# Banks of PSUM assigned by hand, whole accumulators as side work, a shared score bank and x transposed by DMA, in a recurrent attention kernel

## The chip, the cores and the metric

One core of one Trainium2 chip. The time of a kernel is its device time in microseconds. The runs of one kernel lie within 0.5% of their median here. A ratio is the mean time of one kernel's fast runs over that of the other's fast runs of the same rounds, so it is not quite the ratio of the medians quoted beside it. Within a trace, times are counted from the start of the execution.

## The reference

A gate mixes two branches. Branch B is a layer norm and a two-layer MLP; it takes the first 108 us and the change leaves it alone. Branch A runs through the sequence in 64 segments of 32 rows, one after the other, because each hands eight rows of memory to the next:

```python
for s in range(64):
    h = concatenate([mem, x[:, 32*s : 32*s+32]])          # 8 + 32 rows of 512
    q, k, v = h @ Wq, h @ Wk, h @ Wv                      # 32 heads of 128
    p = softmax(where(mask, q @ k.T * 128**-0.5, -1e9))   # 40 x 40 per head
    o = (p @ v) @ Wo
    mem = o[:, :8]                                        # needed by the next s
    outs.append(o[:, 8:])
return g * concatenate(outs) + (1 - g) * B(x)             # g = sigmoid(x . gate_w)
```

## The kernel before

A step of the loop is one segment; a tile is four steps (128 rows of x). TensorE works on 32 rows at a time, with four column tiles side by side. Such a block holds the 8 memory rows and the first 24 rows of the segment. The last 8 rows of each of four segments ("left-over", names with L) do not depend on the memory; they are projected a tile ahead, as side work, which fills TensorE wherever a step would wait. The matmuls write into PSUM, of which the kernel uses eight banks. One is S, for the scores; the other seven go round in the order of the calls:

```python
pb = loop.enter_context(tc.tile_pool(name="pb", bufs=7, space=PSUM))
ps = loop.enter_context(tc.tile_pool(name="ps", bufs=1, space=PSUM))
def bank(shape, dtype=FP32):
    return pb.tile(shape, dtype, tag="b", name="b")

def x_tr(T, x_sb):                                # x tile T, transposed on TensorE
    xp = bank([P, KC, P], BF16)
    for kc in range(KC):
        nc.tensor.transpose(xp[:, kc, :], x_sb[:, kc * P:(kc + 1) * P], ident[:])
    def ev():                                     # VectorE copies it out, GpSimd picks GL
        ...

def filler(T):                                    # side work of a tile, in units of four matmuls
    if T + 1 < NT:
        for vb in range(2):
            yield from left_v(T + 1, vb)          # its result goes through DRAM to VL
        for hf in range(2):
            for t in range(2):
                yield from left_qk(T + 1, t, hf)
    if T >= 1:
        yield from wo_left(T - 1)
        yield from out_units(T - 1)               # also x_tr(T + 2), its load just before
```

The step, with cuts:

```python
            if s >= 1:
                prep_q(s)                         # GpSimd: QL -> QT columns 32:40
                x_mul(s - 1)                      # GpSimd: Px = E * R
            ...                                   # q, k: five banks, VectorE transposes,
                                                  # ScalarE (GpSimd for the third) casts to QT, KT
            scores(S, s)                          # TensorE, needs all of QT
            ...                                   # E = exp(S) on ScalarE, first sums sm
            run_fill(5)                           # five side units
            ...                                   # Pm; four banks Um <- Pm V, then VL
            sr = bank([P, NG, 32])                # late sums, and R = 1/sr on VectorE (1.75 us)
            run_fill(2)
        for half in range(2):
            wp = bank([P, 256])                   # Wo, two halves
            ...
        if live and s >= 1:
            av_x(s - 1)                           # four more banks <- Px V, then VL
        run_fill(1)
        if s + 1 < nseg:
            aT = bank([P, KC, M])                 # new memory, transposed by matmuls with Sel
            ...
            nc.vector.tensor_copy(out=hn[:, :, 0:M], in_=aT[:])
            S_next = mask_mm()                    # mask of the next step into S
        run_fill(1)
```

## Time and profile before

| | before |
|---|---|
| median | 921.3 us (three runs, 918.32 to 922.12) |
| TensorE busy | 832.7 us, 90% of the span |
| first step begins | 138.7 us |
| the four steps of an inner tile (medians) | 11.99, 12.02, 12.16, 11.54 us |
| last step begins, to the end | 25.3 us |

The row of steps is read from the timeline: a step begins with its first matmul of Wq with hT. The lines that carry the argument are in the prediction. A reader of such lines should take the distance between the starts of two matmuls, not their durations: matmuls are pipelined, and their ends are modelled.

### The profile page before, as it was taken

The numbers are of one execution on the slowest core, as the hardware profiler recorded it, in microseconds if no ns is written. First come the engines' busy times: TensorE is split into PE (matmuls) and PEld (weight loads), VectorE is DVE, ScalarE is ACT, GpSimd is POOL, SyncE is SP. The second block draws the span as 40 slices with busy tenths as digits, with TensorE's granted clock in tenths as the row PEclk, the third lists the DMA queues.
The fourth block names the chain that finished last, engine by engine and source line by source line (L and its number), as shares of the span: only waits on it lengthen the run. The fifth ranks groups of instructions, "written<-read, shape, count | busy, mean of one in ns | idle before, by whom it ended". The sixth has DMA issues, their size and how long they took to land.

```text
span 920.6 us, 49285 instructions
## 1 busy us (share of the span) xinstructions
PE 832.7 (90%) x22481; PEld 519.9 (56%) x22481; DVE 502.2 (55%) x999; ACT 443.2 (48%) x1252; POOL 257.1 (28%) x599
## 2 busy tenths in 40 slices
PE   1899738899999999999999999999999999999996
PEld 1566414555556566565656555656555566655554
DVE  4722214655556565556565656565656565655553
ACT  2666404454545445554544454555455545444453
POOL 1000172333333322333332323232323232323221
PEclk9999959999999999999999999999999999999998
DMA  9970001100000000010101000000000000000000
GB/s 281 421 260 1 7 1 31 27 9 26 15 27 15 27 16 26 10 32 10 32 5 37 5 27 14 28 14 23 19 21 21 15 27 15 27 15 21 10 4 17
DMA packets 29829, 37.77 MB, mean 41 GB/s; under 512 B 3592, under 2 KB 27504, under 8 KB 28080
## 3 DMA queue, kind: packets, MB, share of 16 engines
q1 hardware_dynamic: 29440, 34.30, 10.9%
q8 instruction: 178, 2.92, 1.3%
q0 software_dynamic: 176, 0.27, 0.2%
q14 instruction: 35, 0.29, 0.1%
HBM read 28.26 MB, written 6.29 MB: 38 GB/s over the span
## 4 chain that ended last, share of the span: by engine, by line
PE 81%; ACT 7%; issue 3%; DVE 3%; DMA 2%; POOL 2%; SPq 1%; ACTq 0%; POOLq 0%; DVEq 0%
PE b L269 32%; PE b L291 16%; PE b L280 12%; PE b L451 4%; PE bp L172 3%; PE hp L178 3%; ACT E L552 3%; PE b L456 2%; PE S L436 2%; PE b L566 1%; ACT wsb L590 1%; PE b L599 1%; PE b L555 1%; ACT UTT L511 1%; PE S L427 1%
## 5 line engine op out<-in xcount | busy, mean ns | idle before, releaser
L275 DVE STREAM_TRANSPOSE Tt<-b 128x512 f32<-128x512 f32 (+1 forms) x384 | 225.8, 613 | 97.4 <-PE b L269 85.1
L269 PEld LDWEIGHTS <-hT 128*32 128x32 bf16 x5120 | 134.1, 97 | 93.1 <-DVE hT L600 6.3
L291 PE MATMUL b<-Wo_sb,UTT 128*32 128x256 bf16 (+1 forms) x4736 | 166.4, 289 | 1.1 <-ACT UTT L511 0.8
L291 PEld LDWEIGHTS <-UTT 128*32 128x32 bf16 x4736 | 125.3, 98 | 26.9 <-issue 3.1
L269 PE MATMUL b<-Wq_sb,hT 128*32 128x512 bf16 x2048 | 132.9, 379 | 1.3
L280 PE MATMUL b<-Wv_sb,hT 128*32 128x512 bf16 x2048 | 133.9, 380 | 0.0
L269 PE MATMUL b<-Wk_sb,hT 128*32 128x256 bf16 (+1 forms) x3072 | 133.3, 308 | 0.0
L497 POOL TENSOR_TENSOR Px<-E,R 128x256 bf16<-128x256 bf16 x64 | 43.1, 674 | 258.1 <-DVE R L571 254.4
L571 DVE RECIPROCAL R<-b 128x256 f32<-128x256 f32 x64 | 112.0, 1749 | 4.2 <-PE b L567 4.2
L536 ACT CAST KT<-Tt 128x256 bf16<-128x256 f32 (+1 forms) x192 | 87.0, 476 | 54.1 <-DVE Tt L275 54.1
L536 POOL CAST QT<-Tt 128x512 bf16<-128x512 f32 x64 | 39.2, 612 | 189.7 <-DVE Tt L275 189.7
L590 ACT CAST wsb<-b 128x256 bf16<-128x256 f32 x66 | 24.6, 372 | 134.3 <-PE b L291 134.3
L536 ACT CAST QT<-Tt 128x512 bf16<-128x512 f32 x64 | 39.6, 618 | 98.7 <-DVE Tt L275 98.7
L511 ACT CAST UTT<-b 128x256 bf16<-128x256 f32 x256 | 77.0, 387 | 12.8 <-PE b L456 10.0
L559 DVE RECIPROCAL R<-b 128x64 f32<-128x64 f32 x64 | 35.7, 557 | 85.1 <-PE b L556 85.1
L280 PEld LDWEIGHTS <-hT 128*32 128x32 bf16 x2048 | 50.7, 96 | 28.2
L451 PEld LDWEIGHTS <-V 32*128 32x128 bf16 x4096 | 36.2, 91 | 50.8 <-DVE Pm L561 29.0
L600 DVE CAST hT<-b 128x32 bf16<-128x32 f32 x63 | 12.0, 191 | 90.3 <-PE b L599 90.3
L570 ACT CAST UTT<-b 128x64 bf16<-128x64 f32 x128 | 20.9, 215 | 77.5 <-PE b L456 77.5
L178 PE MATMUL hp<-yT,w_sb 128*128 128x256 bf16 (+1 forms) x352 | 52.5, 276 | 5.3 <-ACT hTm L179 3.5
L499 POOL TENSOR_TENSOR racc<-racc,R 128x320 f32<-128x320 f32 x64 | 55.1, 862 | 0.0
L179 ACT ACTIVATE hTm<-hp,b_sb 128x256 bf16<-128x256 f32 (+1 forms) x88 | 40.5, 470 | 29.2 <-PE hp L178 29.0
(110 smaller groups left out, 1087.1 us busy)
## 6 DMA issues: line engine op xcount, KB each, us to landing
Wq_sb<-in_A_Wq_dram SPq DMA_DIRECT2D x4, 1024.0 KB
Wk_sb<-in_A_Wk_dram SPq DMA_DIRECT2D x4, 1024.0 KB
Wv_sb<-in_A_Wv_dram SPq DMA_DIRECT2D x4, 1024.0 KB
Wo_sb<-in_A_Wo_dram SPq DMA_DIRECT2D x4, 1024.0 KB
vd<-vt SPq DMA_DIRECT2D x32, 128.0 KB
VL<-vd SPq DMA_DIRECT2D x256, 16.0 KB
out_dram<-o SPq DMA_DIRECT2D x16, 128.0 KB
xc<-in_A_x_dram SPq DMA_DIRECT2D x15, 128.0 KB
```

What stands on the lines that cost most here:

```text
L178: nc.tensor.matmul(hp[:rows, :], lhsT=w1_sb[:, kc, fc * P:fc * P + rows], rhs=yT[:, kc, :], start=(kc == 0), stop=(kc == KC - 1))
L179: nc.scalar.activation(out=hTm[:rows, fc, :], in_=hp[:rows, :], func=ACTF.Gelu_apprx_tanh, bias=b1_sb[:rows, fc:fc + 1], scale=1.0)
L269: nc.tensor.matmul(bk[32 * j:32 * j + 32, 0:n], lhsT=G[:, kc, :], rhs=W5[t][:, kc, h0:h1, j, :], start=(kc == 0), stop=(kc == KC - 1), til ...
L275: nc.vector.transpose(out=Tt[:, 0:n], in_=bk[:, 0:n])
L280: nc.tensor.matmul(bk[32 * j:32 * j + 32, :], lhsT=G[:, kc, :], rhs=Wv5[:, kc, 4 * vb:4 * vb + 4, j, :], start=(kc == 0), stop=(kc == KC - ...
L291: nc.tensor.matmul(bk[32 * g:32 * g + 32, :], lhsT=ut[:, i, j, c0:c0 + 32], rhs=Wo_sb[:, 4 * i + j, d0:d1], start=(j == 0 and i < 4), stop ...
L451: nc.tensor.matmul(U[j][:, i, :], lhsT=V[q, i, :], rhs=Pt[q, i, c_main:c_main + n], start=(i == 0), stop=False, skip_group_check=True, til ...
L497: nc.gpsimd.tensor_tensor(out=Px[:, :, 0:32], in0=E[:, :, 16:48], in1=Rr, op=ALU.mult)
L499: nc.gpsimd.tensor_tensor(out=racc[:], in0=racc[:], in1=R[:], op=ALU.add)
L511: nc.scalar.copy(out=UTT[T % 2][:, :, j, c0 + M:c0 + 40], in_=U[:])
L536: (nc.gpsimd.tensor_copy if bi == 2 else nc.scalar.copy)(out=dst, in_=Tv)
L571: nc.vector.reciprocal(out=R[:, 8 * NG:].rearrange("p (i q) -> p i q", q=32), in_=sr[:])
```

## The change

Its intent is to rid TensorE of waits for banks. Every accumulator gets a bank by number: 0 to 4 turn in a ring for the main work, 5 and 6 alternate for side work, and bank 7 holds mask and scores, later the late sums, and then, beside the next mask, the new memory. Side work becomes two whole accumulators in each step, with units placed four, two, one and one (one more in two of the places in step 3). As mask and memory share a bank, the mask moves ahead of the value product. And the transposes of x leave TensorE and VectorE for the DMA.

```diff
-    pb = loop.enter_context(tc.tile_pool(name="pb", bufs=7, space=PSUM))
-    ps = loop.enter_context(tc.tile_pool(name="ps", bufs=1, space=PSUM))
+    pb = loop.enter_context(tc.tile_pool(name="pb", bufs=1, space=PSUM))
+    def bank(k, shape, dtype=FP32):
+        return pb.tile(shape, dtype, tag=f"b{k}", name=f"b{k}")
...
     def x_load(T):
+        xT = cw.tile([P, KC, P], BF16, tag="xT", bufs=3, name="xT")
+        for kc in range(KC):
+            nc.sync.dma_start_transpose(xT[:, kc, :], x2[T * P:(T + 1) * P, kc * P:(kc + 1) * P])
+        xTs[T] = xT
+        GL = cw.tile([P, KC, 32], BF16, tag="GL", name="GL")
+        nc.gpsimd.tensor_copy(out=GL[:]..., in_=xT[:]...)
+        GLs[T] = GL
...
+        if si == 1 and T + 2 < NT:
+            x_load(T + 2)
+        if live:
+            B, S = S_next
+            na, nb, nc_, nd, ne = ring
+            ring = (nd, ne, na, nc_, nb)
             if s >= 2:
                 ux_out(s - 2)
+                flush(act_q)
...
             if s >= 1:
                 prep_q(s)
                 x_mul(s - 1)
...
-            run_fill(5)
+            run_fill(4 + (si == 3))
...
-            sr = bank([P, NG, 32])
+            sr = B[:, 0:NG * 32].rearrange("p (i q) -> p i q", q=32)
...
+        if s + 1 < nseg:
+            S_next = mask_mm()
         if live and s >= 1:
-            av_x(s - 1)
+            av_x(s - 1, (ne, na, nc_, nb))
-        run_fill(1)
+        run_fill(1 + (si == 3))
         if s + 1 < nseg:
-            aT = bank([P, KC, M])
+            aT = S_next[0][:, NG * EW:NG * EW + KC * M].rearrange("p (k m) -> p k m", m=M)
...
-            S_next = mask_mm()
         run_fill(1)
```

More of the change, by code (lines that the diff above doesn't have):

```diff
@@ L57 @@
     g_all = pers.tile([P, NT], FP32)
-    x0_sb = pers.tile([P, Dm], BF16)
     with tc.tile_pool(name="mlpw", bufs=1) as mlpw, \
@@ L101 @@
             nc.sync.dma_start(Wo_sb[:, i:i + hsplit, :], A_Wo[i:i + hsplit].rearrange("h e d -> e h d"))
-        nc.sync.dma_start(x0_sb[:], x2[0:P, :])
         make_identity(nc, ident[:])
@@ L250, with flush, later, side @@
                                     fill=MASK_NEG, base=M, channel_multiplier=-1)
-    pb = loop.enter_context(tc.tile_pool(name="pb", bufs=7, space=PSUM))
-    ps = loop.enter_context(tc.tile_pool(name="ps", bufs=1, space=PSUM))
+    pb = loop.enter_context(tc.tile_pool(name="pb", bufs=1, space=PSUM))
     dr = loop.enter_context(tc.tile_pool(name="dr", bufs=2, space=bass.MemoryType.DRAM))
     cw = loop.enter_context(tc.tile_pool(name="cw", bufs=2))
-    def bank(shape, dtype=FP32):
-        return pb.tile(shape, dtype, tag="b", name="b")
+    def bank(k, shape, dtype=FP32):
+        return pb.tile(shape, dtype, tag=f"b{k}", name=f"b{k}")
+    side_n, side_todo = [0], set()
+    dve_q, act_q = [], []
+    def flush(q, n=1):
+        for _ in range(min(n, len(q))):
+            k, ev = q.pop(0)
+            ev()
+            side_todo.discard(k)
+    def later(q, ev, k):
+        side_todo.add(k)
+        q.append((k, ev))
+    def side(shape, dtype=FP32):
+        side_n[0] += 1
+        while side_n[0] - 2 in side_todo:
+            flush(dve_q)
+            flush(act_q)
+        return bank(5 + side_n[0] % 2, shape, dtype)
     Wq5 = Wq_sb[:].rearrange("p k (h j e) -> p k h j e", h=H, j=4)
@@ L294 @@
     vds, xTs, GLs, wsbs, wsbLs = {}, {}, {}, {}, {}
-    dve_q, act_q = [], []
-    def flush(q, n=1):
-        for _ in range(min(n, len(q))):
-            q.pop(0)()
     def x_load(T):
-        if T == 0:
-            return x0_sb
-        x_sb = cw.tile([P, Dm], BF16, tag="xc", bufs=1, name="xc")
-        nc.sync.dma_start(x_sb[:], x2[T * P:(T + 1) * P, :])
-        return x_sb
-    def x_tr(T, x_sb):
-        xp = bank([P, KC, P], BF16)
-        for kc in range(KC):
-            nc.tensor.transpose(xp[:, kc, :], x_sb[:, kc * P:(kc + 1) * P], ident[:])
-        def ev():
-            xT = cw.tile([P, KC, P], BF16, tag="xT", bufs=3, name="xT")
-            nc.vector.tensor_copy(out=xT[:], in_=xp[:])
-            xTs[T] = xT
-            GL = cw.tile([P, KC, 32], BF16, tag="GL", name="GL")
-            nc.gpsimd.tensor_copy(out=GL[:].rearrange("p k (i c) -> p k i c", c=LEFT),
-                                  in_=xT[:].rearrange("p k (i c) -> p k i c", c=seg)[:, :, :, RIDE:seg])
-            GLs[T] = GL
-        dve_q.append(ev)
+        xT = cw.tile([P, KC, P], BF16, tag="xT", bufs=3, name="xT")
+        for kc in range(KC):
+            nc.sync.dma_start_transpose(xT[:, kc, :], x2[T * P:(T + 1) * P, kc * P:(kc + 1) * P])
+        xTs[T] = xT
+        GL = cw.tile([P, KC, 32], BF16, tag="GL", name="GL")
+        nc.gpsimd.tensor_copy(out=GL[:].rearrange("p k (i c) -> p k i c", c=LEFT),
+                              in_=xT[:].rearrange("p k (i c) -> p k i c", c=seg)[:, :, :, RIDE:seg])
+        GLs[T] = GL
     HF = ((0, H // 2), (H // 2, H))
@@ L326, in left_qk @@
         h0, h1 = HF[hf]
-        bk = bank([P, 512])
+        bk = side([P, 512])
+        side_k = side_n[0]
         for kc in range(KC):
@@ L339, in ev @@
                     nc.gpsimd.tensor_copy(out=KL[T % 2][:, :, :, hh, :], in_=Tv[:, r0:r0 + 8, :].rearrange("p g (s c) -> p g s c", c=LEFT))
-        dve_q.append(ev)
+        later(dve_q, ev, side_k)
         yield
     def left_v(T, vb):
-        bk = bank([P, 512])
+        bk = side([P, 512])
+        side_k = side_n[0]
         for kc in range(KC):
@@ L361, in ev @@
                         nc.sync.dma_start(VL[T % 2][r0:r0 + LEFT].rearrange("p s g e -> p s (g e)"), src[j, hh])
-        act_q.append(ev)
+        later(act_q, ev, side_k)
         yield
     def wo_left(T):
-        bk = bank([P, Dm])
+        bk = side([P, Dm])
+        side_k = side_n[0]
         for u in range(8):
@@ L375, in ev @@
             wsbLs[T] = w
-        act_q.append(ev)
+        later(act_q, ev, side_k)
         yield
     def out_units(T):
-        ob = bank([P, Dm])
+        ob = side([P, Dm])
+        side_k = side_n[0]
         for si in range(SPT):
@@ L384, in out_units @@
         yield
-        if T + 3 < NT:
-            x_tr(T + 3, x_load(T + 3))
-            yield
-        if T not in wsbLs:
-            flush(act_q, 9)
         for si in range(SPT):
@@ L397, in ev, with side_work @@
             nc.sync.dma_start(out2[T * P:(T + 1) * P, :], o_sb[:])
-        dve_q.append(ev)
+        later(dve_q, ev, side_k)
         yield
-    def filler(T):
-        if T + 1 < NT:
-            for vb in range(2):
-                yield from left_v(T + 1, vb)
-            for hf in range(2):
-                for t in range(2):
-                    yield from left_qk(T + 1, t, hf)
-        if T >= 1:
+    def side_work(T, si):
+        if si < 3 and T + 1 < NT:
+            for n in range(2):
+                if si == 0:
+                    yield from left_v(T + 1, n)
+                else:
+                    yield from left_qk(T + 1, n, si - 1)
+        if si == 3 and T >= 2:
+            yield from out_units(T - 2)
+        if si == 3 and T >= 1:
             yield from wo_left(T - 1)
-            yield from out_units(T - 1)
-        elif NT > 2:
-            x_tr(2, x_load(2))
-            yield
     def prep_h(s):
@@ L425, in mask_mm @@
     def mask_mm():
-        S = ps.tile([P, NG, EW], FP32, tag="S", name="S")
-        nc.tensor.matmul(S[:], lhsT=ident[:], rhs=MkA[:].unsqueeze(2).to_broadcast([P, 4, 2, EW]),
+        B = bank(7, [P, 512])
+        S = B[:, 0:NG * EW].rearrange("p (i e) -> p i e", e=EW)
+        nc.tensor.matmul(S, lhsT=ident[:], rhs=MkA[:].unsqueeze(2).to_broadcast([P, 4, 2, EW]),
                          start=True, stop=True, skip_group_check=True)
-        return S
+        return B, S
     def scores(S, s):
@@ L461 @@
     nc.sync.dma_start(m0[:], A_mem0[0])
-    m0p = bank([P, KC, M], BF16)
+    m0p = side([P, KC, M], BF16)
     for kc in range(KC):
@@ L465 @@
     nc.vector.tensor_copy(out=hT[0][:, :, 0:M], in_=m0p[:])
-    x_tr(0, x_load(0))
-    flush(dve_q)
-    x_tr(1, x_load(1))
-    flush(dve_q)
+    x_load(0)
+    x_load(1)
     prep_h(0)
@@ L484 @@
     S_next = mask_mm()
+    ring = (0, 1, 2, 3, 4)
     Es, Rs, Pxs, Vs, Uxs = {}, {}, {}, {}, {}
@@ L489, in run_fill @@
         for _ in range(n):
-            if T + 1 < NT or si >= 2:
-                next(fill, None)
+            next(fill, None)
     def x_mul(s):
@@ L500, in x_mul, with av_x @@
         Pxs[s] = Px
-    def av_x(s):
-        U = [bank([P, NG, 32]) for _ in range(4)]
+    def av_x(s, banks):
+        U = [bank(k, [P, NG, 32]) for k in banks]
         av(U, 32, s, Vs.pop(s), Pxs.pop(s), 0, 32, 24)
@@ L516 @@
         hc, hn = hT[s % NHT], hT[(s + 1) % NHT]
-        if si == 0 and live:
-            fill = filler(T)
         if live:
-            S = S_next
+            fill = side_work(T, si)
+        if si == 1 and T + 2 < NT:
[4 more added lines that the diff above has]
+            ring = (nd, ne, na, nc_, nb)
+            qk_banks = (na, nb, nc_, nd, ne)
             if s >= 2:
                 ux_out(s - 2)
-            if s + 1 < nseg and (s + 1) // SPT in xTs:
+                flush(act_q)
+            if s + 1 < nseg:
                 prep_h(s + 1)
@@ L530 @@
             for bi, (t, h0, h1) in enumerate(BANKS):
-                bk = bank([P, 512])
+                bk = bank(qk_banks[bi], [P, 512])
                 for kc in range(KC):
@@ L538 @@
             Vs[s] = V
-            vb0, vb1 = bank([P, 512]), bank([P, 512])
+            vb0, vb1 = bank(na, [P, 512]), bank(nb, [P, 512])
             for kc in range(KC):
@@ L542 @@
             nc.scalar.copy(out=v_out(V, 0), in_=vb0[:])
-            flush(dve_q)
+            flush(dve_q, 9)
             for kc in range(2):
@@ L553 @@
             nc.scalar.activation(out=E[:, :, 16:EW], in_=S[:, :, 16:EW], func=ACTF.Exp, scale=scale, accum_out=hist[:, s, 1:2])
-            sm = bank([P, NG, 8])
+            sm = bank(nc_, [P, NG, 8])
             nc.tensor.matmul(sm[:], lhsT=BO[:], rhs=E[:, :, 8:16], start=True, stop=False)
@@ L562 @@
                                     in1=R[:, 0:8 * NG].rearrange("p (i q) -> p i q", q=8).unsqueeze(2).to_broadcast([P, NG, 2, 8]), op=ALU.mult)
-            Um = [bank([P, NG, 8]) for _ in range(4)]
+            Um = [bank(k, [P, NG, 8]) for k in (nd, ne, na, nc_)]
             av(Um, 8, s, V, Pm, 8, 0, 0)
-            sr = bank([P, NG, 32])
-            nc.tensor.matmul(sr[:], lhsT=BO[:], rhs=E[:, :, 16:48], start=True, stop=False, skip_group_check=True)
+            sr = B[:, 0:NG * 32].rearrange("p (i q) -> p i q", q=32)
+            nc.tensor.matmul(sr, lhsT=BO[:], rhs=E[:, :, 16:48], start=True, stop=False, skip_group_check=True)
             nc.tensor.matmul(sr[:, :, 24:32], lhsT=BO[:], rhs=E[:, :, 48:56], start=False, stop=True, skip_group_check=True)
@@ L570 @@
                 (nc.scalar.copy if j % 2 else nc.vector.tensor_copy)(out=UTT[Tp % 2][:, :, j, 24 - 8 * sp:24 - 8 * sp + M], in_=Um[j][:])
-            nc.vector.reciprocal(out=R[:, 8 * NG:].rearrange("p (i q) -> p i q", q=32), in_=sr[:])
+            nc.vector.reciprocal(out=R[:, 8 * NG:].rearrange("p (i q) -> p i q", q=32), in_=sr)
             run_fill(2)
@@ L576 @@
                 x_mul(s - 1)
-                av_x(s - 1)
+                av_x(s - 1, (ne, na, nc_, 7))
             else:
@@ L581 @@
             Tp, sp = divmod(s - 2, SPT)
-        wsb = cw.tile([P, Dm], BF16, tag="wsb", bufs=7, name="wsb")
+        wsb = cw.tile([P, Dm], BF16, tag="wsb", bufs=10, name="wsb")
         for half in range(2):
             d = slice(256 * half, 256 * half + 256)
-            wp = bank([P, 256])
+            wp = bank((nb, nd)[half], [P, 256])
             for u in range(8):
@@ L592 @@
             wsbs[s] = wsb
+        if s + 1 < nseg:
+            S_next = mask_mm()
         if live and s >= 1:
-            av_x(s - 1)
-        run_fill(1)
-        if s + 1 < nseg:
-            aT = bank([P, KC, M])
-            for m in range(KC):
-                nc.tensor.matmul(aT[:, m, :], lhsT=wsb[:, m * P:(m + 1) * P], rhs=Sel[:, 0:M], start=(m == 0), stop=True, skip_group_check=True)
-            nc.vector.tensor_copy(out=hn[:, :, 0:M], in_=aT[:])
-            S_next = mask_mm()
-        run_fill(1)
-        if si == SPT - 1:
-            for _ in fill:
-                pass
-    for _ in filler(NT):
-        flush(dve_q, 9)
-        flush(act_q, 9)
+            av_x(s - 1, (ne, na, nc_, nb))
+        run_fill(1 + (si == 3))
+        if s + 1 < nseg:
+            aT = S_next[0][:, NG * EW:NG * EW + KC * M].rearrange("p (k m) -> p k m", m=M)
+            for m in range(KC):
+                nc.tensor.matmul(aT[:, m, :], lhsT=wsb[:, m * P:(m + 1) * P], rhs=Sel[:, 0:M], start=False, stop=True, skip_group_check=True)
+            nc.vector.tensor_copy(out=hn[:, :, 0:M], in_=aT)
+        run_fill(1)
+        for _ in fill:
+            pass
+    flush(act_q, 9)
+    for _ in out_units(NT - 2):
+        flush(dve_q, 9)
+    for _ in wo_left(NT - 1):
+        pass
+    flush(act_q, 9)
+    for _ in out_units(NT - 1):
+        pass
     flush(dve_q, 9)
@@ L620 @@
     nc.vector.tensor_scalar(out=good[:, 1:2], in0=tot[:, 1:2], scalar1=RSUM_MAX, scalar2=None, op0=ALU.is_lt)
-    cnt = bank([1, 1])
+    cnt = side([1, 1])
     nc.tensor.matmul(cnt[:], lhsT=good[:, 0:1], rhs=good[:, 1:2], start=True, stop=True)
```

## The prediction

> **What bounds the kernel now.** I read the page first, for the engine that is full, then the waits, then the timeline of one tile of four steps in the middle of the loop, then the same view of a late step that shows no wait. The page names TensorE:
>
> ```profile
> PE 832.7 (90%) x22481; PEld 519.9 (56%) x22481; DVE 502.2 (55%) x999; ACT 443.2 (48%) x1252; POOL 257.1 (28%) x599
> ...
> PE 81%; ACT 7%; issue 3%; DVE 3%; DMA 2%; POOL 2%; SPq 1%; ACTq 0%; POOLq 0%; DVEq 0%
> ```
>
> The second line is the chain that ended last: TensorE holds four fifths of it, so only TensorE's own work and the gaps in front of it count. The timeline gives the length of a step as the distance between the first Wq matmuls on hT. One tile (four steps) begins at 477.43, 489.40, 501.43, 513.59 and ends at 525.12: 11.97, 12.03, 12.16, 11.53, together 47.69 us. The late step from 883.87 to 895.27 carries all nine side units and no visible gap; I use its 11.40 us as the measure of a step:
>
> ```profile
> 891.02 0.36 PE L451 MATMUL b<-Pm,V 32*128 32x8 bf16 x32
> 891.23 0.23 PE L456 MATMUL b<-Pm,VL 32*128 32x32 bf16 x8
> 891.39 0.28 PE L566 MATMUL b<-E,BO 128*128 128x256 bf16 x1
> ...
> 893.93 0.37 PE L451 MATMUL b<-Px,V 32*128 32x32 bf16 x32
> 894.15 0.24 PE L456 MATMUL b<-Px,VL 32*128 32x32 bf16 x8
> 894.32 0.40 PE L291 MATMUL b<-Wo_sb,UTT 128*32 128x512 bf16 x4
> 894.65 0.26 PE L599 MATMUL b<-Sel,wsb 128*128 128x8 bf16 x4
> 894.76 0.35 PE L427 MATMUL S<-MkA,ident 128*128 128x448 bf16 x1
> 895.04 0.40 PE L382 MATMUL b<-wsb,SelX 128*32 128x512 bf16 x4
> 895.27 1.04 PE L269 MATMUL b<-Wq_sb,hT 128*32 128x512 bf16 x16
> ```
>
> Against it the four ordinary steps lose time in these places (same view):
>
> ```profile
> 497.35 0.27 PE L566 MATMUL b<-E,BO 128*128 128x256 bf16 x1 [0.36 <-ACT UTT L570]
> ```
> ```profile
> 512.02 0.35 PE L451 MATMUL b<-Px,V 32*128 32x32 bf16 x29 [0.35 <-ACT wsb L590]
> ...
> 512.99 0.24 PE L599 MATMUL b<-Sel,wsb 128*128 128x8 bf16 x4 [0.20 <-ACT UTT L511]
> ```
>
> These are matmuls whose operands are ready and whose bank is not: seven banks go round, and every fourth step the late sums, the last value bank and the new memory land on a bank that ScalarE still reads. The list of waits shows each 15 times, once per tile:
>
> ```profile
> PE b L566 <- ACT UTT L570: 5.5, 15, 0.4
> PE b L451 <- ACT wsb L590: 5.3, 15, 0.4
> ```
>
> Measured as distances against the late step: step 1 of a tile loses 0.44 in front of the late sums (0.81 from the first Pm matmul instead of 0.37) and some 0.2 around the second value product; step 2 loses 0.51 in the second value product (511.48 to 512.38, not 0.39) and 0.28 in front of the new memory. Step 0 loses 0.58 to something else: its left-over value matmuls (VL) take 0.81 instead of 0.23, while TensorE's queue works off semaphore waits for the sixteen small VL transfers. Step 3 has no last side unit and pays about 0.13 for it.
>
> **What the Trainium skill says.** "Perfetto Trace Analysis", section "Optimization Strategy", says that the same gap repeating on the engine that should be full can mean that PSUM has no room for the next tile; the 15-fold waits agree. "TensorE: Matmul & The Clock Gate", "The mechanism", says that matmuls on different column tiles run together, some 4 ns apart. Here 16 matmuls of 512 columns take 0.87 us, so a group of four (one side unit) costs 0.217 us: it agrees. "PSUM — Partial Sum Buffer", "The four PSUM rules", says that a starting matmul clears the written bits of the whole bank, so a later one without the start flag overwrites. The new memory beside the mask rests on it, and it must therefore follow the mask; no run of before shows this. "Advanced Engine Details and Errata", "X-Bar Transpose (TRN2)", says that such transposes are as fast as regular DMAs; the trace of before holds none.
>
> **The change, part by part, per tile.**
>
> *PSUM by hand.* I followed each bank to its last reader. The next step's five projection banks are the second Wo bank and the four value banks, which ScalarE copies out at once (4 copies in 1.20 us, done about 0.4 us into the step; the second projection bank is wanted at 0.86). The mask needs bank 7 free of the 1.75 us reciprocal of the late sums: that ends some 0.35 us before Wo does. The fourth value bank is the first Wo half, copied by VectorE right after that reciprocal, in time too. So I expect all bank waits of steps 1 and 2 to go: 0.44 + 0.2 + 0.51 + 0.28, about 1.4 us, and none to replace them.
>
> *x by DMA.* Four transposes on TensorE go (0.33 us per tile), and with them VectorE's 0.41 us copy, which lay beside other work.
>
> *Side work.* Per tile before: 35 units of which the transposes are one. After: 8, 8, 8 and 10, so 34. But only four units lie between the first sums and the first value product in steps 0 to 2. With no unit there at all the late trace has 1.27 us from the sums to that product (878.91 to 880.18, waiting for Pm); with five it has 1.35. Four take about 1.13, so the floor of 1.27 binds: the stage gains 0.08, not 0.22.
>
> *Mask before the value product.* Before, the mask (0.28) and one side unit (0.23) lie between the new memory's matmuls and the next step, and hide VectorE's copy to hT. The step 3 case without the unit shows the path itself: from the last of the four memory matmuls to the first Wq matmul about 0.45 us (524.67 to 525.12). In the late step it is 0.54, so fully hidden. After the change the mask is ahead of it and only one unit is left: 0.025 + 0.1 to switch + 0.22 is shorter than 0.45, so TensorE stands at hT. As the mask's 0.28 is now paid earlier and the tail shrinks from 0.54 to 0.45, each step gets 0.19 us longer. This is the part that eats the gain.
>
> *Sum.* Step 0: 11.40 - 0.08 + 0.19 + 0.58 (VL waits stay) = 12.09. Steps 1 and 2: 11.51 each. Step 3: 11.40 + one unit 0.22 + 0.19 = 11.81. Together 46.92 against 47.69: 0.77 us per tile, 10.8 us for the 14 inner tiles. First tile: its steps were 16.10, 11.96, 13.25, 10.76; the 16.10 waits for the first VL transfer and stays (+0.19), 13.25 holds the landing of x and becomes 11.5, the rest 11.5 and 10.9: 1.9 us less. Last tile and tail: about 0.3 less (a 1.16 us wait for the left-over Wo result goes, ten side units are squeezed into step 63 and two fall behind the loop). Scattered longer steps of before, such as 12.44 and 11.99, come from the same bank order: 0.9 less. Start: two side banks instead of seven before the loop, 0.3 more; the 16.3 us wait for GpSimd's mask building stays, and the first eight transposes hide under it. In all -13.6 us: 907.7. For the risk below I add a little: 909.
>
> **The rivals.**
>
> *GpSimd stands behind the transposes.* The copy to GL is now issued at the head of step 1, in front of the copies for hT and QT and of the Px products. GpSimd runs ahead and will stand there until all four transposes have landed. SP reaches them only after the store of the first left-over values, issued at 486.50 (9.1 us into step 0). Plain issues take 0.30 to 0.36 us each here; if a transpose takes 0.5 and lands 2 us later, the data is there at 13.2, about 1.1 us into step 1. Then GL, hT, QT and Px (0.29 + 0.27 + 0.40 + 1.84) and the QT copy (0.61) end at 4.5, just ahead of the scores at 4.76. If each takes 1 us or more, every microsecond beyond goes to the end 14 times: 1.5 to 3 us per tile, 930 to 950 us. For it: nothing runs between; against it: the skill's sentence and idle DMA queues (0 or 1 tenth).
>
> *A new bank wait.* One of the slacks above (0.35 us at the mask) is misjudged and a wait of 0.3 us appears in every step: +19 us, 928. For it: one fixed map has no spare bank; against it: every last reader found ends earlier.
>
> *More gain than I see.* The hT path overlaps better than I think or the VL semaphore stall (0.58 x 15 = 9 us) falls away with the new order: 895 to 900. Nothing in the diff touches the latter.
>
> **Range and chances.** The counted gain is 1.5%, well inside 2%; faster by over 2% needs 902.9, that is 5 us more than counted, and slower by over 2% needs 939.7, that is over 2 us of stall per tile. So mostly "same", both tails from the rivals, the upper one longer.
>
> **What will show it.** Right: no wait of L566, of the value products or of the new memory for a ScalarE copy; steps near 12.1, 11.5, 11.5, 11.8; a wait of TensorE for hT of 0.1 to 0.2 us in nearly every step; 0.1 us for Pm in three of four. Wrong: GpSimd's GL copy landing over 1.4 us into step 1 and scores late there; a wait of the mask for the reciprocal; step 0 without the VL stall; or an hT path that is longer than 0.45.

## The result

The changed kernel takes 977.16 us (median of four runs, 975.63 to 980.6), before 919.81 in the same rounds; the ratio is 1.063, with a 95% interval of 1.0586 to 1.0674. It is 6.3% slower and gives the right result.

| | before | predicted | after |
|---|---|---|---|
| first step begins | 138.7 | 139.0 | 138.5 |
| step 0 of an inner tile (medians) | 11.99 | 12.09 | 12.37 |
| step 1 | 12.02 | 11.51 | **15.85** |
| step 2 | 12.16 | 11.51 | 11.54 |
| step 3 | 11.54 | 11.81 | 11.83 |
| last step begins, to the end | 25.3 | | 27.8 |

Two of the four steps are right within 0.03 us, one is off by 0.3, and one by more than 4. The page of after, its row of busy times and its chain that ended last:

```profile
PE 857.5 (88%) x22409; PEld 511.9 (53%) x22417; DVE 498.5 (51%) x983; ACT 444.4 (46%) x1252; POOL 256.0 (26%) x599
...
PE 68%; SPq 8%; POOL 6%; DMA 5%; ACT 5%; DVE 4%; issue 4%; POOLq 0%; ACTq 0%; DVEq 0%
```

TensorE's share of the chain fell from 81% to 68%. In its place stand SP's sequencer, GpSimd and DMA, together 19% against 5% before. GpSimd is no busier than before (256.0 us, then 257.1), nor is the main DMA queue (10.6% of its engines' time, then 10.9%); SP is, for a transpose takes it 1.48 us on average in the loop. The list of waits of after shows who stands behind whom:

```profile
POOL GL L320 <- DMA xT<-in_A_x_dram: 171.6, 13, 14.4
...
PE b L436 <- POOL QT L540: 27.3, 14, 2.0
...
PEld L287 <- DVE hT L606: 16.4, 63, 0.4
...
PE b L436 <- POOL QT L421: 13.2, 13, 2.3
```

GpSimd waits for x 13 times, and the scores (L436) wait 13 and 14 times for the two copies to QT that GpSimd does. Once per tile, then. The three bank waits of before (late sums, second value product and new memory, each for ScalarE) are not in this list any more. TensorE's weight loads wait for hT in all 63 steps that get a new memory, 0.26 us each (before: 18 times, 6.3 us in all). In step 2 of the same tile, in the timeline, the distances are those of an undisturbed step:

```profile
536.02 0.36 PE L451 MATMUL b<-Pm,V 32*128 32x8 bf16 x32
536.24 0.23 PE L456 MATMUL b<-Pm,VL 32*128 32x32 bf16 x8
536.40 0.28 PE L570 MATMUL b<-E,BO 128*128 128x256 bf16 x1
...
539.95 0.26 PE L605 MATMUL b<-Sel,wsb 128*128 128x8 bf16 x4
540.13 0.40 PE L287 MATMUL b<-Wk_sb,GL 128*32 128x512 bf16 x4
540.49 0.83 PE L287 MATMUL b<-Wq_sb,hT 128*32 128x512 bf16 x12
```

From the first Pm matmul to the late sums it is 0.38 us (0.81 in step 1 of before). From the first matmul of the new memory to the next step it is 0.54 us (0.45 from the last of the four, as counted), with a side unit of 0.22 between, so TensorE also stands at hT as foreseen. Step 1 is told by the chain in order of time (start, length, what):

```profile
510.50 0.34 SPq L358
...
510.93 1.52 SPq L317
...
512.50 1.22 SPq L317
...
513.77 1.96 SPq L317
...
515.78 2.33 DMA xT<-in_A_x_dram
...
518.25 0.06 POOL GL L320
...
518.70 0.40 POOL QT L421
519.10 0.63 POOL Px L495
519.73 0.27 POOL Px L496
520.00 0.81 POOL racc L497
520.81 0.56 POOL QT L540
...
521.42 0.32 PE b L436 x15
```

L358 is the store of left-over values, the last thing SP has to wait for. Then SP issues four transposes (L317), at 1.2 to 2 us each. The step begins at 513.62, as the issue of the second ends. The data of the last lands at 518.1, GpSimd does its queue in order (GL, hT, QT, the Px products, the running sum, QT), and the second half of the scores begins at 521.42 instead of some 4.9 us into the step, which would be 518.5. What the wait leaves behind shows in the stretches of this step (window, its length, busy time of PE, PEld, DVE, ACT and POOL; then the granted clock, the DMA share and GB/s):

```profile
518.20:521.40 3.20, 0.64 (x24) 0.24 (x17) 0.00 (x0) 0.57 (x2) 3.15 (x8) 0.91 0.25 75
521.40:524.50 3.10, 3.08 (x54) 0.97 (x55) 0.85 (x2) 1.37 (x5) 0.58 (x2) 0.54 0.17 49
```

After 3.2 us with TensorE nearly idle, the next 3.1 us run at a granted clock of 0.54. The Trainium skill, "TensorE: Matmul & The Clock Gate", section "Why this matters for your kernels", warns of idle gaps over about 3 us. Here shorter ones were enough: TensorE waits 0.59 and 1.99 us, with sixteen matmuls of the scores between. In every step 1 of tiles 1 to 13 of this trace the clock falls to 0.5 for 3.4 us (twice that in three of them), and no single wait there is over 2.3 us. This step takes 15.33 us, 3.79 more than step 2. Of these TensorE stands in front of and within the scores for 2.94; the other 0.86 come from the stretch between the end of the scores and the first Pm matmul, which has the same matmuls as in step 2 and runs at half clock.

### The profile page after: what moved, and what is told of

The parts are those of the page before. It is cut to its first block, busy times and chain, and to the rows that moved or that the text cites. A ratio compares the mean times of both kernels' runs of the same rounds, so it can differ in the third digit from the quotient of the medians.

```text
span 973.9 us, 49254 instructions
## 1 busy us (share of the span) xinstructions
PE 857.5 (88%) x22409; PEld 511.9 (53%) x22417; DVE 498.5 (51%) x983; ACT 444.4 (46%) x1252; POOL 256.0 (26%) x599
## 3 DMA queue, kind: packets, MB, share of 16 engines
q1 hardware_dynamic: 37376, 34.30, 10.6%
## 4 chain that ended last, share of the span: by engine, by line
PE 68%; SPq 8%; POOL 6%; DMA 5%; ACT 5%; DVE 4%; issue 4%; POOLq 0%; ACTq 0%; DVEq 0%
PE b L287 25%; PE b L309 13%; PE b L298 8%; SPq L317 6%; DMA xT<-in_A_x_dram 4%; PE b L451 4%; PE bp L170 4%; PE hp L176 4%; PE b L456 2%; DVE R L563 2%; ACT E L556 2%; PE b L436 2%; PE b L427 2%; PE b L559 1%; POOL racc L497 1%
## 5 line engine op out<-in xcount | busy, mean ns | idle before, releaser
L287 PEld LDWEIGHTS <-hT 128*32 128x32 bf16 x5120 | 130.9, 97 | 101.1 <-DVE hT L606 16.4
L309 PE MATMUL b<-Wo_sb,UTT 128*32 128x256 bf16 (+1 forms) x4736 | 164.3, 286 | 1.5 <-ACT UTT L509 0.7
L298 PE MATMUL b<-Wv_sb,hT 128*32 128x512 bf16 x2048 | 138.6, 390 | 0.0
L298 PEld LDWEIGHTS <-hT 128*32 128x32 bf16 x2048 | 51.2, 97 | 28.2
L436 PE MATMUL b<-QT,KT 128*32 128x40 bf16 x2048 | 28.4, 182 | 40.5 <-POOL QT L540 27.3
L287 PE MATMUL b<-Wq_sb,GL 128*32 128x512 bf16 x512 | 45.6, 491 | 16.9 <-POOL GL L320 16.9
L436 PEld LDWEIGHTS <-KT 128*32 128x32 bf16 x2048 | 26.8, 95 | 58.3 <-issue 45.8
```

The source lines that it names most:

```text
L287: nc.tensor.matmul(bk[32 * j:32 * j + 32, 0:n], lhsT=G[:, kc, :], rhs=W5[t][:, kc, h0:h1, j, :], start=(kc == 0), stop=(kc == KC - 1), til ...
L298: nc.tensor.matmul(bk[32 * j:32 * j + 32, :], lhsT=G[:, kc, :], rhs=Wv5[:, kc, 4 * vb:4 * vb + 4, j, :], start=(kc == 0), stop=(kc == KC - ...
L309: nc.tensor.matmul(bk[32 * g:32 * g + 32, :], lhsT=ut[:, i, j, c0:c0 + 32], rhs=Wo_sb[:, 4 * i + j, d0:d1], start=(j == 0 and i < 4), stop ...
L436: nc.tensor.matmul(S[32 * j:32 * j + 32, i, M:M + 40], lhsT=KT[:, h, :], rhs=QT[:, h, :], start=False, stop=True, skip_group_check=True, t ...
```

## The experiments

Theory A: GpSimd executes in order, and its copy to GL now stands in front of what the scores need; it waits there until SP has issued four slow transposes and the data has landed. Theory B: transposes by DMA disturb the step by themselves, wherever GpSimd stands. Theory C: the new side work or the bank map makes the stall. In the diffs of this section the comments are added here, and lines between the changed ones are left out.

| run | edit against | median us | before in the same rounds | ratio (95%) |
|---|---|---|---|---|
| e1_gl_late | after | 917.17 | 920.5 | 0.9964 (0.9941 to 0.9987) |
| e2_x_early | after | 915.87 | 920.5 | 0.9948 (0.9925 to 0.9971) |
| e3_pe_tr | after | 927.5 | 920.5 | 1.0082 (1.0056 to 1.0109) |
| e4_before_dma | before | 921.76 | 920.5 | 1.0008 (0.9982 to 1.0034) |
| e5_half | after | 926.96 | 920.87 | 1.0073 (1.0037 to 1.011) |
| e6_double | after | 1017.1 | 920.87 | 1.1048 (1.1011 to 1.1085) |
| e7_order | e2_x_early | 896.35 | 920.87 | 0.9742 (0.9719 to 0.9765) |
| e8_one | after | 915.38 | 920.87 | 0.9937 (0.992 to 0.9953) |
| e9_vl | e7_order | 890.85 | 920.8 | 0.9688 (0.9661 to 0.9716) |
| e10_all | e9_vl | 890.04 | 920.8 | 0.9679 (0.9652 to 0.9706) |

All ten gave right results. Each median is of four runs.

**e1_gl_late: the copy to GL later**

```diff
         xTs[T] = xT                # end of x_load: the transposes stay in it
+
+    def gl_copy(T):                # the copy to GL, cut off from x_load
+        xT = xTs[T]
...
         if si == 1 and T + 2 < NT:
             x_load(T + 2)
+        if si == 2 and T + 2 < NT:
+            gl_copy(T + 2)
```

> The changed kernel, with only GpSimd's copy to GL moved from the head of step 1 of a tile (straight behind the issue of the four DMA transposes) to the head of step 2. Theory A (GpSimd stands in its own order behind the landing of the transposes, so the copies for QT come late and the scores with them): step 1 falls from about 15.4 to 11.54 us, the 61 us that the fourteen step 1s have over 11.54 go, total about 916 us. Theory B (the transposes themselves disturb the step, through the DMA queues, the clock or the memory, wherever GpSimd stands): step 1 stays above 14 us and the total above 955. Theory C (the two side accumulators of step 1 and the hand-made bank map make the stall): no change, 977.

Measured: 917.17 us, and step 1 has a median of 11.54. The transposes themselves were no faster here. The timelines of SP and of GpSimd of this run, in the same step of the same tile (it begins at 483.68):

```profile
481.00 6.98 SPq L317 DMA_TRANSPOSE xT<-in_A_x_dram  x4
```
```profile
487.36 0.61 POOL L547 CAST QT<-Tt 128x512 bf16<-128x512 f32 x1 [3.75 <-DVE Tt L293]
490.75 0.29 POOL L323 COPY GL<-xT 128x128 bf16<-128x128 bf16 x1 [2.79 <-DMA xT<-in_A_x_dram]
```

SP spends 6.98 us on the four, more than in the step of after. But the QT copy now goes first, at 3.7 us into the step, and GpSimd waits 2.79 us for x afterwards, which delays nothing. One moved copy takes back 60 us, and the granted clock behind the scores of step 1 is 1.00 again. Theory A holds, B and C fall: transposes, side work and bank map are all unchanged.

**e2_x_early: transposes and copy at step 0**

```diff
-        if si == 1 and T + 2 < NT:
+        if si == 0 and T + 2 < NT:
             x_load(T + 2)
```

> The changed kernel, with the whole x_load (transposes and GL copy, still together) issued at the head of step 0 of a tile in place of step 1. SP then has only the previous tile's transfers ahead of it and can run the transposes during steps 2 and 3 of the tile before, so they have landed when GpSimd comes to GL. Theory A: about 916 us, all steps between 11.5 and 12.4. Theory B: still over 955, the stall only moves to another step. A variant of A in which transposes are simply too slow (over 10 us) would leave a stall in step 0.

Measured: 915.87 us; the steps have medians of 12.37, 11.54, 11.54 and 11.83. GpSimd does not wait for x at all in the trace of this run. SP has nothing ahead of the transposes that waits for this tile, and has issued them long before. So it is not the place of the copy in GpSimd's queue alone that counts, but this place together with what SP has to wait for first.

**e3_pe_tr: x on TensorE again**

```diff
+        if si == 3 and T + 2 < NT:
+            yield from x_tr(T + 2)      # four transposes through a side bank, VectorE copies out
```

(with a plain load of x in step 1 in place of the DMA transposes)

> The changed kernel with x transposed on TensorE again: a plain load in step 1, four transposes as one more side unit in step 3, through a side bank; bank map, side work and mask order as changed. Theory A: as the run with the late GL copy plus 14 x 0.33 us = 4.6 us, so about 920 us; the other three parts of the change together are then worth about nothing against before (within 1%). Theory C: 977, for the stall has nothing to do with the transposes.

Measured: 927.5 us. The stall of step 1 is gone (11.54), as theory A has it and C does not. The total missed the expectation by 7 us: step 3 is 12.80 us long, not 12.2. I put that down to my edit. Three side accumulators in one step share two banks, and the list of waits shows the transposes behind VectorE's reading of the output accumulator, 12 times, 0.6 us at the longest and 7.3 us in all. So the run says less than hoped about what the other parts are worth; e1 and e2 say it.

**e4_before_dma: the transposes alone, in the kernel before**

```diff
-            x_tr(T + 3, x_load(T + 3))
+            x_load(T + 3)               # DMA transposes, then the copy to GL
             yield
```

> The kernel before with this one part of the change alone: x by DMA transposes, in the place where before loaded and transposed it (with the output units, step 3 of a tile), GL copy directly behind. SP has nothing ahead of them that waits, so they should land long before GpSimd comes by. Theory A: 913 to 919 us, 1 to 6 us under before (13 x 0.33 us of TensorE work and the wait for x in step 2 go). Theory B: over 950.

Measured: 921.76 us, no change, a little over the range expected. There is no stall of the inner tiles, so theory B falls again. Step 3 gains 0.45 us, more than the 0.33 of the transposes (11.09 from 11.54), but step 0 loses 0.2 (12.21 from 11.99) and the first tile takes 54.3 us instead of 52.1. Transposing x by DMA was worth nothing by itself. The 0.2 of step 0 lies in its VL product, to which e9 comes back.

**e5_half and e6_double: half and one and a half times the transposes**

```diff
# e5_half: two of the four at the head of step 0, two at step 1 as changed
+        if si == 0 and T + 2 < NT:
+            x_half(T + 2, 0, 2)
# e6_double: the first two issued twice
-        for kc in range(KC):
+        for kc in (0, 1, 0, 1, 2, 3) if T >= 2 else range(KC):
```

> The changed kernel with two of the four transposes of a tile issued at the head of step 0 and the other two, with GpSimd's copy to GL behind them, at the head of step 1 as changed: the same work, half of it between the store of the left-over values and GpSimd's copy. Theory A: two transposes take SP 2.4 to 3.3 us instead of 4.9 to 6.9, they land 1.1 to 1.8 us into step 1 instead of about 4.6, and as GpSimd's chain behind them has room for about 1.2 us, the stall shrinks to 0 to 0.6 us: step 1 between 11.5 and 12.2, total 918 to 926 us. A fixed cost per tile of going through the crossbar at all would leave most of the 61 us: over 945.

> The changed kernel with six transposes per tile in place of four (the first two are issued twice; the result stays right). Theory A: each further one holds SP for 1.23 us or more and GpSimd for as long, one for one, so step 1 grows by 2.5 to 3.5 us to about 18.3, total about 977 + 14 x 2.7 = 1015 us (1005 to 1030). If the stall were not set by SP's issue of the transposes, two more would change nothing.

Measured: 926.96 and 1017.1 us. By the number of transposes in front of GpSimd's copy, step 1 has a mean over tiles 1 to 13 of 12.25 us (two), 16.05 (four, after) and 18.81 (six). From four to six it grows by 2.76, that is 1.4 us for each, about what a transpose takes SP on average in this run's loop (1.37 us; the median over the run is 1.22). From two to four it grows by 3.8, more than two transposes take, and there the half clock joins. The start of the left-over scores comes later by 2.7 us from two to four and by 2.6 from four to six, so the lateness itself grows evenly. The stretch from there to the first Pm matmul takes 0.95 us more than in an undisturbed step in after and 0.04 more in e5, on average; in the e5 step that I looked at, 1.4 us late, the matmuls behind the scores keep their full speed. The half run came out just over its range, because some tiles still stall (14.64 us at the worst).

**e8_one: one transpose of 128 x 512**

```diff
-        for kc in range(KC):
-            nc.sync.dma_start_transpose(xT[:, kc, :], x2[T * P:(T + 1) * P, kc * P:(kc + 1) * P])
+        nc.sync.dma_start_transpose(xT[:], x2[T * P:(T + 1) * P, :])
```

> The changed kernel with one transpose instruction of 128 x 512 per tile in place of four of 128 x 128, in the same place. It measures what the 1.23 us of SP per transpose are for. If they are per instruction, SP is done after 1.3 us, the data lands before GpSimd's chain is late, and the total is about 917 us. If they are per block transposed, the one instruction takes SP about 4.9 us, the stall stays and the total is 970 to 980 us. The result may come out wrong if the instruction lays out the four blocks in another order than the kernel reads; the times stand all the same.

Measured: 915.38 us, with the right result. The lines of the tile xT, first of after, then of this run (count; duration in ns, least, median and most):

```profile
L317 SPq DMA_TRANSPOSE xT<-in_A_x_dram x64: 1102/1232/2388, 111.7 to 827.7; - x64
```
```profile
L316 SPq DMA_TRANSPOSE xT<-in_A_x_dram x16: 1195/1278/2063, 111.5 to 767.2; - x16
```

Four times the data costs SP 1.28 us, hardly more than 1.23. The cost is of the instruction, at these sizes, not of the blocks. A single one lands before GpSimd's chain is late, with everything in its place as changed, and the stall is gone.

**e7_order: side units placed anew**

On top of e2:

```diff
-            run_fill(4 + (si == 3))     # behind the first sums
+            run_fill(5)
-            run_fill(2)                 # behind the late sums
+            run_fill(1 + (si == 3))
-        run_fill(1 + (si == 3))         # between value product and new memory
+        run_fill(si == 3)
-        run_fill(1)                     # behind the new memory
+        run_fill(2)
```

> The run with x_load at step 0, with the side units of a step placed anew: five behind the first sums (all steps), one behind the late sums (two in step 3), none between value product and new memory (one in step 3), two behind the new memory. It tests what the prediction says of the order of mask and memory: TensorE stands at hT because only one unit follows the memory, and stands for Pm because only four follow the sums. If so, steps 1 and 2 go from 11.54 to about 11.2 us and step 3 from 11.83 to about 11.7, total about 915.9 - 14 x 1.2 = 899 us, and under 902.9 it is faster than before by over 2%. If the waits for hT and Pm are not what these steps lose, the total stays at 916.

Measured: 896.35 us, ratio 0.9742: faster than before by over 2%. Steps 1 and 2 have a median of 11.15 us, step 3 has 11.69, step 0 has 11.94. Step 2 of the same tile, in the timeline:

```profile
498.57 0.26 PE L605 MATMUL b<-Sel,wsb 128*128 128x8 bf16 x4
498.75 0.61 PE L287 MATMUL b<-Wk_sb,GL 128*32 128x512 bf16 x8
499.20 1.04 PE L287 MATMUL b<-Wq_sb,hT 128*32 128x512 bf16 x16
```

In step 2 of after (above) four matmuls lie behind the new memory; here it is eight, two units. The next step follows 0.45 us after they begin, which is their own length (two times 0.217), so the wait for hT is covered. The same eight units do the same work in 0.39 us less. Where a side unit stands decides whether it fills a gap or lengthens the step.

**e9_vl: the order of the small transfers**

```diff
-                for j in range(4):
+                for j in (2, 3, 0, 1):
                     for hh in range(4):
...
```

> The run with the new order of side units, with the sixteen VL transfers issued for the quadrants in the order 2, 3, 0, 1 in place of 0, 1, 2, 3. TensorE's queue reads quadrant 0 first. The trace of that run shows its left-over value product in step 0 behind sixteen semaphore waits in four groups of about 0.23 us: the eight semaphores of the DMA lanes, each twice, first for an earlier and then for a later count. Theory: if the quadrants that are read first are loaded last, the first two groups wait for the later counts and the other two fall away, so step 0 goes from 11.94 to about 11.5 us, total 896.4 - 15 x 0.45 = 889.5 us. Rival: the stall is the transfers' landing or the fetch of the instructions, then nothing changes, 896.

Measured: 890.85 us; step 0 of the same tile has 11.47 us. The left-over value product of step 0, in e7 and then in this run:

```profile
472.01 0.63 PE L456 MATMUL b<-Pm,VL 32*128 32x32 bf16 x3
472.88 0.20 PE L456 MATMUL b<-Pm,VL 32*128 32x32 bf16 x5 [0.23 <-issue]
```
```profile
469.89 0.45 PE L456 MATMUL b<-Pm,VL 32*128 32x32 bf16 x8
```

In both, SP had issued the last of the transfers over 25 us before. So it is not the data that TensorE's queue stood for; I read it as the working off of the waits one by one, which an order with the later transfers first shortens. The records of the waits in the traces bear this out: in e7 the queue works off 16 semaphore waits in front of this product, in groups of four that come 0.23 us apart or a little more; in this run there are 8. Two groups fewer is what was expected, and step 0 is shorter by 0.46 us at the median. No run changed the number of waits in another way. The loop's length shrinks by about half a microsecond per tile for four swapped numbers.

**e10_all: e9 with one transpose per tile**

```diff
-        for kc in range(KC):
-            nc.sync.dma_start_transpose(xT[:, kc, :], x2[T * P:(T + 1) * P, kc * P:(kc + 1) * P])
+        nc.sync.dma_start_transpose(xT[:], x2[T * P:(T + 1) * P, :])
```

> The run with the VL order turned, and one transpose of 128 x 512 per tile in place of four. The transposes are already off every path that sets the end, so this should change the time by no more than 1 us either way: 888 to 890 us if the VL order works, 895 to 897 if not.

Measured: 890.04 us against 890.85, as good as the same: off the path, four instructions cost no more than one. This version beats both kernels, with a ratio of 0.9679 to before.

## Why the prediction was wrong

**The step that failed** is the first rival, which I named and then counted as unlikely: "if a transpose takes 0.5 and lands 2 us later, the data is there at 13.2, about 1.1 us into step 1". The 907.7 us that I counted rest on this case and hold no stall; only 1.3 us were added for the risk. The 0.5 was taken from the 0.30 to 0.36 us of plain issues in the trace of before and from the skill's sentence that transposes are as fast as regular DMAs. A transpose took SP 1.23 us at the median and up to 2.39. The four took 6.07 us in the step shown (5.5 to 6.9 in the loop, not 2) and the last landed about 1.1 us after the end of its issue (517.0 to 518.1), some 4.5 us into the step instead of 1.1. The landing was overestimated (2 us), the issue underestimated by a factor of 2.5 at the median and about 3 in the loop. The chain behind it was right, link by link: GL, hT, QT, Px, QT, scores, as e1, e2 and e8 show, each of which cuts one link.

The rival's price was too low as well. I gave it 930 to 950 us. The stall is 61 us in all: the sum over the fourteen step 1s of what they have over 11.54. That is 2.3 in the first tile and 4.5 on average in tiles 1 to 13, where the price allowed 1.5 to 3. Two things were missing. The left-over scores alone come 3.35 us late there on average, as four issues take 5.5 us or more. And I had not counted the half clock after the gap, 0.86 us in the step shown and 0.95 on average. Had I taken the "1 us or more" case as the likely one, 977 would still have lain outside its price.

**What was right.** *Bank waits*: all of steps 1 and 2 go and none replaces them in the trace of after (step 2: 11.54 for 11.51; step 1 the same in e1 and e2). *Mask before the value product*: TensorE stands at hT; a step ends 0.45 us after the last matmul of the new memory, and e7 takes the loss back by moving units alone. *Floor of Pm*: step 2 of after has 1.27 us from the sums to the first Pm matmul, with four units, as foreseen. *Step 3*: 11.83 for 11.81. *Start*: GpSimd's building of the masks hides the first eight transposes; the first step begins at 138.5.

**Mis-sized terms.** *Step 0*: 12.37 instead of 12.09. I held the VL stall at 0.58 us and wrote that nothing in the diff touches it; from the first Pm matmul to the late sums it is now about 1.2 us, not 0.96, a stall of some 0.8. The queue of before waits for 14 semaphores there, that of after for 16. Why two more must be waited for I did not test, but e4, with only the transposes changed, waits for 16 and has most of the loss too, and e9 shows that the time hangs on the order of these transfers. Over 14 tiles these 0.28 us are 4 us. *Tail*: 27.8 us from the start of the last step, before 25.3; I had expected the last tile and tail together 0.3 us shorter, and the three steps before the last are 1.2 us shorter. No run looks into that.

**What the gain came to.** Without the stall (e1, e2, e8), the change as written is worth 0.4 to 0.6%, not the 1.5% counted; the difference is step 0 and the tail, and the small scatter of the steps, which the prediction put down to the order of the banks and which did not go away.

## What to carry to other kernels

When an instruction is put into an in-order queue, ask what the queue's next instructions are for and when the awaited data lands; that is the issue time of everything before it on the other queue plus the landing, not the size of the transfer. An idle engine shows nothing of this: GpSimd waits 116 us for x in e8 and loses nothing, and 172 in after and loses 61, and only the chain tells them apart. And before moving work to another engine to save its time, look at where the filler stands: the same eight units, placed behind the first sums and behind the new memory, were worth 19.5 us (915.87 to 896.35), as much as all bank waits of the inner tiles were counted for (1.4 us by 14).

## What the Trainium skill lacked or had wrong

- "Advanced Engine Details and Errata", section "X-Bar Transpose (TRN2)", says that transposing DMAs are as fast as regular ones. For small tiles the issue is not: 1.23 us of SP for 128 x 128 (two-byte elements) against 0.30 to 0.36 us for a plain DMA, medians of the traces of before and after, and 1.28 us for 128 x 512. Within the loop single ones took up to 2.4 us; what lengthens them is open.
- No page that I read gives the price of semaphore waits in front of one TensorE instruction. Sixteen of them, on transfers issued over 25 us before, stand in step 0 where TensorE's queue loses some 0.8 us, and each further group of four comes 0.23 us after the last or a little more; with the transfers in another order there are eight, and e9 gained 5.5 us in all.
- "TensorE: Matmul & The Clock Gate", section "Why this matters for your kernels", puts the gap to avoid at about 3 us. In the step 1s of tiles 1 to 13 of after the clock fell to 0.5 with no single wait over 2.3 us; what the limit is these runs do not show.
